# Adding the experts' parts to the output in DRAM by accumulating transfers, with the first product of each half scaled on ScalarE

## The chip, the cores and the metric

One core of one Trainium2 chip. The metric is the device time of one execution in microseconds (us), as the median of several executions. The kernel before takes 1807.9 us (four runs, 1805.82 to 1808.64). The chip is one of several, so each series of runs has its own runs of the kernel before.

Names: PE is TensorE (PEld its weight loads), DVE is VectorE, ACT is ScalarE, POOL is GpSimd, SP is SyncE.

## The reference

```python
# attention without softmax: batch 8, heads 8, sequence 576, head size 64
kv  = einsum('bhsd,bhse->bhde', k, v)
o   = einsum('bhsd,bhde->bhse', q, kv)
x   = o / sqrt(mean(o*o, -1) + 1e-6) * g_norm        # -> 4608 rows x 512
# four experts, all of them applied to every row
p   = domain_probs / (domain_probs.sum(-1) + 1e-9)
out = zeros(4608, 512)
for e in range(4):
    h    = maximum(x @ w1[e], 0)                     # 512 -> 1024
    out += p[:, e:e+1] * (h @ w2[e])                 # 1024 -> 512
```

The change concerns the last line, the sum over the experts.

## The kernel before

The rows are worked in 9 blocks of 512. A step is one expert and one block, so there are 36 steps: first all nine blocks with expert 0, then with expert 1, and so on. Both products of a step are made with seven instead of eight block products (a Strassen form), which costs DVE and POOL many additions. At a *change of expert* the sums of the next expert's weights (`w1y` and `big`, 128x256 each) come on top of the usual additions of the step.

The kernel keeps its own list scheduler. Every operation has a key (its place in the work), a cost for each engine that may do it, and the buffers that it needs. The scheduler simulates the engines, gives each addition to whichever of DVE and POOL can take it first, and emits the instructions in that order. Additions carry a flag, so that the simulation runs them one at a time. That flag does not reach the program: in the emitted program only data dependencies order an addition of one engine against one of the other.

```python
def either(n):
    return {"DVE": 0.17 + 0.00108 * n, "POOL": 0.1 + 0.0025 * n}

def combine(key, cost, out_, a, b, op, reads, writes):      # every addition of the Strassen forms
    plan.add(
        key, cost,
        lambda eng: adder(eng).tensor_tensor(out=out_(), in0=a(), in1=b(), op=op),
        reads=reads, writes=writes, port=True,              # port: one at a time, in the simulation
    )
...
def down(s, e, c):                                          # h @ w2[e], for block c in step s
    h = hidden.pop(s)
    base = s + 1.0
    acc, made = {}, set()
    for i in range(NR):
        acc[i] = Buf("small", f"acc{s}_{i}")
        if e:                                               # load the sum of the experts so far
            load(
                base + (i % 2) * 0.5 - 0.35, acc[i], lambda i=i: acc[i].ap[:],
                out_kept[c, i][:], 256, reads=[kept[c, "o", i]],
            )
            made |= {(i, 0), (i, 1)}

    def merge(key, ps, i, half):                            # 14 a step, all on DVE
        ...
            if fresh:
                nc.vector.tensor_scalar_mul(
                    out=acc[i].ap[:, cols], in0=ps.ap[:, 0:HN], scalar1=prob
                )
            else:
                nc.vector.scalar_tensor_tensor(
                    out=acc[i].ap[:, cols], in0=ps.ap[:, 0:HN], scalar=prob,
                    in1=acc[i].ap[:, cols], op0=ALU.mult, op1=ALU.add,
                )
        ...
    ...                                                     # store: from SP, to out_kept, at the last expert to out
            plan.add(
                key, pe(4, HN), product, reads=[h[m], w2f[e][m]], writes=[ps]
            )
```

Of the kernel before, what the change touches and what calls it, by code (L numbers as in the profile page):

```python
# [10 lines left out]
ALU = mybir.AluOpType  # L11
# [179 lines left out]
def kernel(  # L191
# [30 lines left out]

    nc = tc.nc
# [49 lines left out]
    out_kept = {  # L273
        (c, i): dram.tile([P, DM], F32, tag=f"o{c}_{i}", name=f"o{c}_{i}")
        for c in range(NCH) for i in range(NR)
    }

    plan = Plan()

    def pe(products, columns, passes=2):  # L280
        return {"PE": passes * products * (2 * columns + 6) / 2400 + 0.003}
# [423 lines left out]
    hidden = {}  # L705
    last = []
# [107 lines left out]
    def down(s, e, c):  # L814
        h = hidden.pop(s)
        base = s + 1.0
        acc, made = {}, set()
        for i in range(NR):
            acc[i] = Buf("small", f"acc{s}_{i}")
            if e:  # L820
                load(
                    base + (i % 2) * 0.5 - 0.35, acc[i], lambda i=i: acc[i].ap[:],
                    out_kept[c, i][:], 256, reads=[kept[c, "o", i]],
                )
                made |= {(i, 0), (i, 1)}

        def merge(key, ps, i, half):
            cols = slice(half * HN, (half + 1) * HN)

            def fn(eng):  # L830
                fresh = (i, half) not in made
                made.add((i, half))
                prob = p_all[:, c * NR + i, e:e + 1]
                if fresh:
                    nc.vector.tensor_scalar_mul(  # L835
                        out=acc[i].ap[:, cols], in0=ps.ap[:, 0:HN], scalar1=prob
                    )
                else:
                    nc.vector.scalar_tensor_tensor(  # L839
                        out=acc[i].ap[:, cols], in0=ps.ap[:, 0:HN], scalar=prob,  # L840
                        in1=acc[i].ap[:, cols], op0=ALU.mult, op1=ALU.add,
                    )

            plan.add(key - 0.4, {"DVE": 0.5}, fn, reads=[ps, probs], parts=[acc[i]])

        def store(key, i):
            if e < E - 1:
                kept[c, "o", i] = Buf(None, f"o{c}_{i}")
                plan.add(
                    key, SPC,  # L850
                    lambda eng: nc.sync.dma_start(out=out_kept[c, i][:], in_=acc[i].ap[:]),
                    reads=[acc[i]], writes=[kept[c, "o", i]], kb=256,
                )
                return

            def final(eng):
                if c < B:
                    rows = out[c * S:c * S + NT, :].rearrange("(p r) d -> p r d", r=NR)
                    nc.sync.dma_start(out=rows[:, i, :], in_=acc[i].ap[:])
                    return  # L860
                for bb in range(2):
                    end = (2 * i + bb + 1) * S
                    nc.sync.dma_start(
                        out=out[end - REM:end, :], in_=acc[i].ap[bb * REM:(bb + 1) * REM, :]
                    )

            plan.add(key, SPC, final, reads=[acc[i]], kb=256)

        for t in range(2):
            banks = {}  # L870
            for j, m in enumerate(ORDER):
# [8 lines left out]
                def product(eng, m=m, t=t, ps=ps):  # L880
# [8 lines left out]
                plan.add(  # L889
                    key, pe(4, HN), product, reads=[h[m], w2f[e][m]], writes=[ps]  # L890
                )
                if m in (1, 2):
                    merge(key, ps, t, 0)
                elif m in (6, 3):
                    merge(key, ps, t, 1)
                elif m in (5, 7):
                    merge(key, ps, 2 + t, 1)
                elif m == 4:
                    merge(key, ps, 2 + t, 0)
# [68 lines left out]
```

## Time and profile before

| what | before |
|---|---|
| time, median | 1807.9 us (the profiled execution: 1805.55 us) |
| span of the profile | 1803.8 us |
| PE busy | 1788.7 us, 99% |
| DVE, ACT, POOL busy | 1010.0, 614.3, 582.0 us |
| waits of PE, all | 10.1 us, 8.3 of them in the first 80 us |
| end of PE to end of span | 4.55 us |

PE is the bound, and it loses time where it waits. Three stretches matter below, the three changes of expert. The windows view of the kernel before: the columns are the stretch, its length, then the busy time (and number of instructions) of PE, PEld, DVE, ACT and POOL, the granted PE clock, the share of the DMA engines and GB/s.

```profile
500.00:560.00 60.00, 58.75 (x394) 54.08 (x393) 36.48 (x67) 17.82 (x42) 30.99 (x23) 1.00 0.40 132
...
930.00:970.00 40.00, 40.00 (x270) 37.52 (x269) 24.43 (x45) 12.29 (x27) 14.58 (x11) 1.00 0.55 180
...
1350.00:1410.00 60.00, 60.00 (x402) 56.15 (x401) 37.18 (x62) 20.03 (x43) 30.24 (x16) 1.00 0.51 170
```

Look at the first figure after the length: PE loses 1.25 us at the change to expert 1 and nothing at the other two.

### The profile page before, as it was taken

The numbers are of one execution on the slowest core, as the hardware profiler recorded it, in microseconds if no ns is written. First come the engines' busy times: TensorE is split into PE (matmuls) and PEld (weight loads), VectorE is DVE, ScalarE is ACT, GpSimd is POOL, SyncE is SP. The second block draws the span as 40 slices with busy tenths as digits, with TensorE's granted clock in tenths as the row PEclk, the third lists the DMA queues.
The fourth block names the chain that finished last, engine by engine and source line by source line (L and its number), as shares of the span: only waits on it lengthen the run. The fifth ranks groups of instructions, "written<-read, shape, count | busy, mean of one in ns | idle before, by whom it ended". The sixth has DMA issues, their size and how long they took to land.

```text
span 1803.8 us, 31919 instructions
## 1 busy us (share of the span) xinstructions
PE 1788.7 (99%) x12626; PEld 1667.9 (92%) x12626; DVE 1010.0 (56%) x1757; ACT 614.3 (34%) x1345; POOL 582.0 (32%) x447
## 2 busy tenths in 40 slices
PE   8999999999999999999999999999999999999998
PEld 8899999999989999999999999999999999999997
DVE  5765565556565555555565555555565555555553
ACT  3534444443232333333333333333332333333331
POOL 4855555546445211111155111111144211111112
PEclk9999999999999999999999999999999999999999
DMA  9855454323343333343445333334444334344321
GB/s 229 250 188 138 129 170 154 113 97 141 134 141 129 129 129 129 129 128 123 157 147 169 118 120 127 124 123 129 152 161 167 122 124 129 129 129 129 128 96 35
DMA packets 163286, 247.78 MB, mean 137 GB/s; under 512 B 51009, under 2 KB 92225, under 8 KB 163137
## 3 DMA queue, kind: packets, MB, share of 16 engines
q1 hardware_dynamic: 163136, 245.75, 42.6%
q8 instruction: 99, 1.62, 0.4%
q14 instruction: 51, 0.41, 0.1%
HBM read 172.56 MB, written 73.14 MB: 136 GB/s over the span
## 4 chain that ended last, share of the span: by engine, by line
PE 97%; DVE 1%; POOL 1%; SPq 1%; DMA 0%; ACT 0%; issue 0%; POOLq 0%; DVEq 0%; ACTq 0%
PE u L745 44%; PE db L882 30%; PE ab L882 18%; PE ab L539 1%; PE ab L521 1%; PE ab L549 1%; PE ab L506 1%; SPq L310 1%; PE ab L588 0%; DMA big<-in_v_dram 0%; PE u L927 0%; POOL big L304 0%; DVE big L304 0%; POOL rt L458 0%; PE ab L603 0%
## 5 line engine op out<-in xcount | busy, mean ns | idle before, releaser
L304 POOL TENSOR_TENSOR big<-big,big 128x1024 f32<-128x1024 f32 x136 | 323.7, 2391 | 1005.9 <-DVE big L304 815.0
L882 PE MATMUL db<-big,big 128*128 128x256 f32 x2520 | 594.6, 379 | 0.7 <-POOL big L304 0.7
L882 PEld LDWEIGHTS db<-big,big 128*128 128x128 f32 x2520 | 455.7, 190 | 50.8 <-POOL big L304 1.1
L745 PEld LDWEIGHTS u<-xf,big 128*128 128x128 f32 x3600 | 470.2, 192 | 20.9 <-issue 0.9
L761 ACT ACTIVATE snap<-u 128x256 f32<-128x256 f32 x756 | 290.1, 384 | 585.3 <-PE u L745 497.2
L745 PE MATMUL u<-xf,big 128*128 128x128 f32 x3600 | 486.1, 276 | 0.1
L769 DVE TENSOR_TENSOR big<-u,snap 128x256 f32<-128x256 f32 x756 | 314.8, 422 | 240.0 <-PE u L745 124.0
L304 DVE TENSOR_TENSOR big<-big,big 128x1024 f32<-128x1024 f32 x292 | 372.9, 1278 | 31.4 <-ACT big L728 13.3
L745 PE MATMUL u<-xf,w1y 128*128 128x128 f32 x2700 | 357.1, 275 | 0.7 <-DVE big L769 0.6
L882 PE MATMUL ab<-big,big 128*128 128x256 f32 x1512 | 357.4, 379 | 0.0
L745 PEld LDWEIGHTS u<-xf,w1y 128*128 128x128 f32 x2700 | 334.6, 192 | 5.8 <-DVE big L769 1.0
L882 PEld LDWEIGHTS ab<-big,big 128*128 128x128 f32 x1512 | 273.3, 190 | 29.8
L839 DVE SCALAR_TENSOR_TENSOR small<-db,p_all,small 128x256 f32<-128x256 f32 x243 | 117.2, 482 | 247.6 <-PE db L882 247.3
L761 ACT ACTIVATE big<-u 128x256 f32<-128x256 f32 x252 | 96.8, 384 | 413.3 <-PE u L745 410.9
L728 ACT ACTIVATE big<-big 128x1024 f32<-128x1024 f32 x144 | 151.8, 1054 | 71.7 <-DVE big L304 60.3
L839 DVE SCALAR_TENSOR_TENSOR small<-ab,p_all,small 128x256 f32<-128x256 f32 x189 | 91.1, 482 | 149.5 <-PE ab L882 149.4
L835 DVE TENSOR_SCALAR small<-db,p_all 128x256 f32<-128x256 f32 x72 | 34.7, 482 | 70.3 <-PE db L882 63.9
L458 POOL TENSOR_TENSOR rt<-ss,mhalf 128x8 f32<-128x8 f32 (+1 forms) x40 | 66.1, 1652 | 3.3
L304 POOL TENSOR_TENSOR xf<-xf 128x128 f32<-128x128 f32 (+1 forms) x74 | 47.8, 656 | 17.6 <-DVE xf L304 15.2
L449 DVE TENSOR_REDUCE ss<-small 128x8 f32<-128x512 f32 (+1 forms) x40 | 27.1, 679 | 22.4 <-ACT small L444 22.3
L454 POOL TENSOR_SCALAR ss<-ss 128x8 f32<-128x8 f32 (+1 forms) x40 | 9.3, 232 | 77.2 <-DVE ss L449 75.8
L745 PE MATMUL u<-small,big 128*128 128x128 f32 x216 | 33.6, 280 | 0.6 <-ACT snap L761 0.5
(83 smaller groups left out, 744.3 us busy)
## 6 DMA issues: line engine op xcount, KB each, us to landing
xf<-x SPq DMA_DIRECT2D x108, 512.0 KB, 3.4
o<-small SPq DMA_DIRECT2D x108, 256.0 KB, 2.1
small<-o SPq DMA_DIRECT2D x108, 256.0 KB, 4.2
xf<-x_h SPq DMA_DIRECT2D x81, 256.0 KB, 3.4
xf<-x SPq DMA_DIRECT2D x81, 256.0 KB, 3.6
x<-xf SPq DMA_DIRECT2D x36, 512.0 KB, 3.2
big<-in_moe_w_dram SPq DMA_DIRECT2D x32, 512.0 KB, 5.8
small<-in_q_dram SPq DMA_DIRECT2D x72, 128.0 KB, 4.1
```

What stands on the lines that cost most here:

```text
L304: lambda eng: adder(eng).tensor_tensor(out=out_(), in0=a(), in1=b(), op=op),
L310: key, SPC, lambda eng: nc.sync.dma_start(out=dst(), in_=src), reads=reads,
L449: lambda eng: nc.vector.reduce_sum(out=ss.ap[0:n, :], in_=rows(sq), axis=AX.X),
L458: nc.gpsimd.tensor_tensor(out=rt.ap[0:n, :], in0=ss.ap[0:n, :], in1=mhalf[0:n, :], op=ALU.pow)
L506: nc.tensor.transpose(bank.ap[:, rs], qt.ap[:, rs], ident[:])
L728: lambda eng: nc.scalar.activation(out=b.ap[:], in_=b.ap[:], func=ACT.Relu),
L745: nc.tensor.matmul(ps.ap[:, u * P:(u + 1) * P], lhsT=w1f[e][m][mm][1]()[:, u * P:(u + 1) * P], rhs=views[m][mm][1](), start=(mm in (1, 2, ...
L761: lambda eng: nc.scalar.activation(out=where(), in_=ps.ap[:, 0:HN], func=ACT.Copy),
L769: lambda eng: nc.vector.tensor_tensor(out=block(whole, a, t), in0=src.ap[:, 0:HN], in1=add_.ap[:], op=ALU.add),
L835: nc.vector.tensor_scalar_mul(out=acc[i].ap[:, cols], in0=ps.ap[:, 0:HN], scalar1=prob)
L839: nc.vector.scalar_tensor_tensor(out=acc[i].ap[:, cols], in0=ps.ap[:, 0:HN], scalar=prob, in1=acc[i].ap[:, cols], op0=ALU.mult, op1=ALU.add,)
L882: nc.tensor.matmul(ps.ap[:, 0:HN], lhsT=four(h[m])[:, kt // 2, t, kt % 2, :], rhs=w2f[e][m].ap[:, kt * HN:(kt + 1) * HN], start=(m in (1, ...
```

## The change

The intent is to free the DMA queues and DVE. An expert's part is no longer added to the sum on DVE after loading that sum; it is scaled, and then added to the output in DRAM by the transfer itself. Such transfers are issued from POOL. Since no half starts from a loaded sum, the first product of each half is only a scaling, which ACT can do. A third thing comes with it, in the last hunk: in the second half of a step's down product (`h @ w2[e]`), products 1 and 2 may not come before product 5 (`m == 5`) of the first half (`after=second[-1:]`). Without that line the scheduler finds no order at all for the changed kernel: it stops with "no operation can start".

```diff
-                load(
-                    base + (i % 2) * 0.5 - 0.35, acc[i], lambda i=i: acc[i].ap[:],
-                    out_kept[c, i][:], 256, reads=[kept[c, "o", i]],
-                )
...
+            if fresh:
+                plan.add(
+                    key - 0.4, act(HN),
+                    lambda eng: nc.scalar.activation(
+                        out=acc[i].ap[:, cols], in_=ps.ap[:, 0:HN], func=ACT.Copy, scale=prob()),
+                    reads=[ps, probs], writes=[first], parts=[acc[i]],
+                )
+                return
...
             def fn(eng):
+                for parts, dst in where:
+                    if e:
+                        nc.gpsimd.dma_start(out=dst, in_=acc[i].ap[parts, :], accum_op=ALU.add)
+                    else:
+                        nc.sync.dma_start(out=dst, in_=acc[i].ap[parts, :])
...
-                plan.add(
-                    key, pe(4, HN), product, reads=[h[m], w2f[e][m]], writes=[ps]
-                )
+                op = plan.add(
+                    key, pe(4, HN), product, reads=[h[m], w2f[e][m]], writes=[ps],
+                    after=second[-1:] if t and m in (1, 2) else (),
+                )
+                if m == 5:
+                    second.append(op)
...
-                    merge(key, ps, t, 0)
+                    merge(key, ps, t, 0, m == 1)
```

More of the change, by code (lines that the diff above doesn't have):

```diff
@@ L271 @@
         for c in range(NCH) for m in ("h0", "h1", 1, 2, 3, 4, 5, 6, 7)
-    }
-    out_kept = {
-        (c, i): dram.tile([P, DM], F32, tag=f"o{c}_{i}", name=f"o{c}_{i}")
-        for c in range(NCH) for i in range(NR)
     }
@@ L705 @@
     hidden = {}
+    summed = {}
     last = []
@@ L816, in down @@
         base = s + 1.0
-        acc, made = {}, set()
-        for i in range(NR):
-            acc[i] = Buf("small", f"acc{s}_{i}")
-            if e:
-                load(
-                    base + (i % 2) * 0.5 - 0.35, acc[i], lambda i=i: acc[i].ap[:],
-                    out_kept[c, i][:], 256, reads=[kept[c, "o", i]],
-                )
-                made |= {(i, 0), (i, 1)}
-        def merge(key, ps, i, half):
-            cols = slice(half * HN, (half + 1) * HN)
-            def fn(eng):
-                fresh = (i, half) not in made
-                made.add((i, half))
-                prob = p_all[:, c * NR + i, e:e + 1]
-                if fresh:
-                    nc.vector.tensor_scalar_mul(
-                        out=acc[i].ap[:, cols], in0=ps.ap[:, 0:HN], scalar1=prob
-                    )
-                else:
-                    nc.vector.scalar_tensor_tensor(
-                        out=acc[i].ap[:, cols], in0=ps.ap[:, 0:HN], scalar=prob,
-                        in1=acc[i].ap[:, cols], op0=ALU.mult, op1=ALU.add,
-                    )
-            plan.add(key - 0.4, {"DVE": 0.5}, fn, reads=[ps, probs], parts=[acc[i]])
@@ L846, in store, with merge, prob @@
-        def store(key, i):
-            if e < E - 1:
-                kept[c, "o", i] = Buf(None, f"o{c}_{i}")
+        acc = {i: Buf("small", f"acc{s}_{i}") for i in range(NR)}
+        def merge(key, ps, i, half, fresh):
+            cols = slice(half * HN, (half + 1) * HN)
+            first = halved[i, half]
+            def prob():
+                return p_all[:, c * NR + i, e:e + 1]
+            if fresh:
                 plan.add(
-                    key, SPC,
-                    lambda eng: nc.sync.dma_start(out=out_kept[c, i][:], in_=acc[i].ap[:]),
-                    reads=[acc[i]], writes=[kept[c, "o", i]], kb=256,
+                    key - 0.4, act(HN),
+                    lambda eng: nc.scalar.activation(
+                        out=acc[i].ap[:, cols], in_=ps.ap[:, 0:HN], func=ACT.Copy, scale=prob()),
+                    reads=[ps, probs], writes=[first], parts=[acc[i]],
@@ L853, in store @@
                 )
                 return
-            def final(eng):
-                if c < B:
-                    rows = out[c * S:c * S + NT, :].rearrange("(p r) d -> p r d", r=NR)
-                    nc.sync.dma_start(out=rows[:, i, :], in_=acc[i].ap[:])
-                    return
-                for bb in range(2):
-                    end = (2 * i + bb + 1) * S
-                    nc.sync.dma_start(
-                        out=out[end - REM:end, :], in_=acc[i].ap[bb * REM:(bb + 1) * REM, :]
-                    )
@@ L867, in store @@
-            plan.add(key, SPC, final, reads=[acc[i]], kb=256)
+            plan.add(
+                key - 0.4, {"DVE": 0.5},
+                lambda eng: nc.vector.scalar_tensor_tensor(
+                    out=acc[i].ap[:, cols], in0=ps.ap[:, 0:HN], scalar=prob(),
+                    in1=acc[i].ap[:, cols], op0=ALU.mult, op1=ALU.add,
+                ),
+                reads=[ps, probs, first], parts=[acc[i]],
+            )
+        halved = {(i, f): Buf(None, f"acc{s}_{i}_{f}") for i in range(NR) for f in range(2)}
@@ new lines, in rows, with store, fn @@
+        def rows(i):
+            if c < B:
+                return [(slice(0, P), out[c * S:c * S + NT, :].rearrange(
+                    "(p r) d -> p r d", r=NR)[:, i, :])]
+            ends = [(2 * i + bb + 1) * S for bb in range(2)]
+            return [
+                (slice(bb * REM, (bb + 1) * REM), out[ends[bb] - REM:ends[bb], :])
+                for bb in range(2)
+            ]
+        def store(key, i):
+            where = rows(i)
+            was = summed.get((c, i))
+            now = summed[c, i] = Buf(None, f"o{s}_{i}")
+            def fn(eng):
+                for parts, dst in where:
[3 more added lines that the diff above has]
+                        nc.sync.dma_start(out=dst, in_=acc[i].ap[parts, :])
+            plan.add(
+                key, {"POOL": 1.2 * len(where)} if e else {"SP": 0.55 * len(where)}, fn,
+                reads=[acc[i]] + ([was] if was else []), writes=[now], kb=256,
+            )
@@ L869, in down @@
+        second = []
         for t in range(2):
@@ L887, in product @@
                         )
-                plan.add(
-                    key, pe(4, HN), product, reads=[h[m], w2f[e][m]], writes=[ps]
-                )
+                op = plan.add(
+                    key, pe(4, HN), product, reads=[h[m], w2f[e][m]], writes=[ps],
+                    after=second[-1:] if t and m in (1, 2) else (),
+                )
+                if m == 5:
+                    second.append(op)
                 if m in (1, 2):
-                    merge(key, ps, t, 0)
+                    merge(key, ps, t, 0, m == 1)
                 elif m in (6, 3):
-                    merge(key, ps, t, 1)
+                    merge(key, ps, t, 1, m == 6)
                 elif m in (5, 7):
-                    merge(key, ps, 2 + t, 1)
+                    merge(key, ps, 2 + t, 1, m == 5)
                 elif m == 4:
-                    merge(key, ps, 2 + t, 0)
+                    merge(key, ps, 2 + t, 0, True)
             store(base + 0.5 * (t + 1), t)
```

## The prediction

> **What bounds the kernel now.** I read the page's busy shares first, then its slices, then the chain that ended last, then the waits of TensorE alone, and last the groups that the change touches. From the page:
>
> ```profile
> PE 1788.7 (99%) x12626; PEld 1667.9 (92%) x12626; DVE 1010.0 (56%) x1757; ACT 614.3 (34%) x1345; POOL 582.0 (32%) x447
> ...
> PEclk9999999999999999999999999999999999999999
> DMA  9855454323343333343445333334444334344321
> ...
> PE 97%; DVE 1%; POOL 1%; SPq 1%; DMA 0%; ACT 0%; issue 0%; POOLq 0%; DVEq 0%; ACTq 0%
> PE u L745 44%; PE db L882 30%; PE ab L882 18%; PE ab L539 1%; PE ab L521 1%; PE ab L549 1%; PE ab L506 1%; SPq L310 1%; PE ab L588 0%; DMA big<-in_v_dram 0%; PE u L927 0%; POOL big L304 0%; DVE big L304 0%; POOL rt L458 0%; PE ab L603 0%
> ```
>
> The reader sees a TensorE that is never free, at the full granted clock, while every other engine has 44% or more of the span to spare and the DMA engines have more than half, except in the first slices. Busy matmuls alone would not prove that PE has no slack, so I looked for its waits. The waits of PE list 13 pairs, about 11.4 us in all; limited to stretches of time they lie before 80 us (attention starting up), 1.1 us between 500 and 600 us, 0.7 us near the end, and none at all from 100 to 500 us and from 600 to 1760 us. The windows and the chain in order of time say the same:
>
> ```profile
> 600.00:700.00 100.00, 100.00 (x674) 93.82 (x673) 54.71 (x94) 31.59 (x70) 14.07 (x6) 1.00 0.40 129
> ...
> 1779.33 0.02 issue
> 1779.35 1.06 ACT big L728
> 1780.41 0.03 POOLq L304
> 1780.44 1.20 POOL big L304
> 1781.64 0.04 issue
> 1781.68 1.99 PE db L882 x8
> 1783.68 1.73 PE ab L882 x8
> 1785.40 6.91 PE db L882 x32
> 1792.31 6.92 PE ab L882 x32
> 1799.23 0.02 issue
> 1799.26 0.48 DVE small L839
> ```
>
> The stream is at its own rate. Eight records of a down product take 1.73 us (0.216 each), sixteen of an up product take 1.78 us in the same view (0.111 each). The groups count 4032 down records and 7056 up records: 4032 x 0.216 + 7056 x 0.111 = 871 + 783 = 1654 us of the 1803.8. The rest is attention, the filler matmuls at the start, the 11 us of waits and the end. One of the 36 steps (an expert and a block of rows) is 1654 / 36 = 46 us of PE.
>
> **What the Trainium skill says.** The page "DMA: Bandwidth & Descriptors", section "SWDGE vs HWDGE vs iDMA", says that accumulating in a transfer can only be had from GpSimd, whose cores write the descriptors in software. The trace before has no transfer from POOL (all data goes on SP's queue), so it neither agrees nor disagrees. The same page, "Anatomy of one DMA", fits a GpSimd transfer with 2.0 us plus bytes over 436 GB/s: 2.6 us for 256 KB and 2.3 us for 128 KB. SP's plain stores of those sizes landed in 2.1 to 2.9 us and 2.3 us here, so the size of that figure is plausible; what reading and adding in DRAM costs on top is not in it. "Perfetto Trace Analysis", section "DMA Instruction — SWDGE (GPSIMD)", says that the profiled end of such an instruction is the last descriptor written, not the data landed, so POOL's rows will show its own time, not the transfer's. "SBUF — State Buffer", section "SBUF: two separate sides", says that GpSimd and VectorE exclude each other when VectorE runs a two-port mode, or has two SBUF inputs while GpSimd reads SBUF; it warns of descriptor writing that starves. The trace before cannot test it for descriptors.
>
> **The change part by part.** The groups and issues it touches:
>
> ```profile
> L304 POOL TENSOR_TENSOR big<-big,big 128x1024 f32<-128x1024 f32 x136 | 323.7, 2391 | 1005.9 <-DVE big L304 815.0
> L761 ACT ACTIVATE snap<-u 128x256 f32<-128x256 f32 x756 | 290.1, 384 | 585.3 <-PE u L745 497.2
> L304 DVE TENSOR_TENSOR big<-big,big 128x1024 f32<-128x1024 f32 x292 | 372.9, 1278 | 31.4 <-ACT big L728 13.3
> L839 DVE SCALAR_TENSOR_TENSOR small<-db,p_all,small 128x256 f32<-128x256 f32 x243 | 117.2, 482 | 247.6 <-PE db L882 247.3
> ...
> o<-small SPq DMA_DIRECT2D x108, 256.0 KB, 2.1
> small<-o SPq DMA_DIRECT2D x108, 256.0 KB, 4.2
> ```
>
> *Merges.* Of the 504 merges of a down product (14 per step), 8 per step are the first into their half and go to ACT: 288. DVE loses 288 x 0.482 = 139 us. ACT gains 288 evictions of 128x256 out of PSUM, which take 0.384 us in the group of the same shape: 111 us. A bank is then free about 0.1 us sooner. PE does not wait for banks in the stretches above, so this is worth nothing by itself.
>
> *Work moved.* The order of instructions of the two kernels shows that the scheduler uses DVE's free time: 51 of the 136 large 128x1024 adds go from POOL to DVE, and some forty small ones. POOL loses 51 x 2.391 = 122 us and about 19 us of small ones; DVE gains 51 x 1.278 = 65 us and about 12 us. DVE comes to 1010 - 139 + 65 + 12 = about 950 us, ACT to 725 us, POOL's arithmetic to about 440 us. In a step of expert 1 to 3 POOL keeps one large add where it had three.
>
> *Transfers.* 108 loads of the partial output (28 MB) and 108 stores to a scratch tensor go from SP's queue; 40 plain stores stay (expert 0), and 120 accumulating transfers come to POOL (96 of 256 KB, 24 of 128 KB). I take 1 us of POOL for each, an estimate from the first-byte time of about 1 us on the DMA page (the schedule itself assumes 1.2): 120 us beside the work it lost. In a step that is four issues, about 4 to 5 us, and one add of 2.4 us, in 46 us. Each adding transfer waits for the previous one of the same rows; that one is nine steps, over 400 us, older. Its staging tile is used again about two steps later, some 90 us after the issue. Both are far from any limit.
>
> *PE.* Same 6540 matrix instructions in both programs, same shapes; the order is identical up to the 511th, where the first down products start, so the start-up with most of the waits is untouched. None of the three parts above is on the path that sets the end. Sum for the body: 0.
>
> *The closing step* is different. Before, from the end of PE at 1799.23 to the end of the span are 4.57 us: 0.48 of merge, a short issue, the landing, the closing. The last block is the one whose rows go out in two 64-row transfers, so after the change POOL issues four transfers at the end in order: two for row 1, whose merge is done 1.2 us before PE ends, and two for row 3, whose last product ACT evicts 0.4 us after PE ends. At 0.7 to 1.2 us each (an estimate from the 1 us above, less for half the rows) POOL is done 1.8 to 3.6 us after PE; landing 2.5 to 3.5 us with the addition; closing 0.6. That is 4.9 to 7.7 us where 4.57 were: +0.3 to +3.1, middle +1.7. Against it, the wait of 0.7 us on POOL at 1781 should shrink, as the chain of adds and relus before it gets two DVE adds in place of two POOL adds. Net about +1 us.
>
> **The rivals.**
> 1. *POOL becomes slow or blocked.* If an issue costs 2 us or more, or descriptor writing is starved by DVE (busier with two-input adds), the add that POOL keeps, which an early product of each down part needs, is late in every step. For it: POOL runs in order, and that add stands right behind four issues. Against it: POOL idles 86% of these stretches, and each step has several us between that add and the product. Waits of 0.5 to 1.5 us in 27 steps would make 1822 to 1850 us.
> 2. *ACT or DVE late for the up products.* ACT's merges stand between the evictions that the up products wait for. Against it: 0.384 us each, ACT at 40%, and the scheduler placed them with costs close to the measured ones. At 0.2 us in some 36 steps: +5 to +8 us.
> 3. *The saved traffic pays.* The loads removed could have slowed the block loads of the next step. Against it: PE waits for no transfer after 40 us, so these were hidden; the gain is 0. Even removing every PE wait gives 11 us, 0.6%.
> 4. *Adding transfers are far slower than plain ones.* Hidden in the body; in the closing step 5 to 10 us more.
>
> **Range and chances.** 1808.56 plus 1 is about 1810 us. Downwards only the scatter of the runs before (1805.82 to 1808.64) and a few us of waits are to be had: 1803. Upwards rivals 2 and 4 together give 1822. Faster by over 2% would need 36 us from a TensorE that has 11 us of waits: 1%. Slower by over 2% needs rival 1 in its strong form: 4%.
>
> **What would show it.** Right: PE at 99% with 12626 records, no wait of PE between 100 and 1760 us above 3 us in all, ACT near 725 us, DVE near 950 us, POOL below 460 us of arithmetic, SP without loads of the partial output, a new queue for POOL's transfers, and 5 to 8 us from the last matmul to the end. Wrong: PE waits on POOL or ACT that return in each step of the later experts, or a mean of the large POOL or DVE add far above 2391 and 1278 ns, or issues of POOL over 2 us; then the step "sum for the body: 0" has failed.

## More of the kernel before

One more line turned out to matter, and I had not looked at it before I predicted. It is from the view of the program's closing line, POOL's drain (a wait of the engine for itself at the end); the three numbers are the shortest, median and longest duration in ns, then the first and last start.

```profile
L963 POOLq DRAIN  x3: 39/77/2456, 1781.7 to 1803.5; - x3
```

The longest, 2.46 us from 1781.7, covers POOL's last addition, which takes about 2.35 us. The drain itself costs next to nothing here.

## The result

The changed kernel takes 1822.24 us (four runs, 1821.33 to 1823.74) where the kernel before took 1807.9. The ratio is 1.0082, with a 95% interval of 1.0065 to 1.0099. It is correct. Ratios here are the mean time of one kernel's fast runs over that of the other's of the same rounds, so they are not quite the ratio of the medians. The loss is below 2%, but the 14.3 us are real, and they lie just outside the range.

Line numbers differ a little from kernel to kernel: L304, L300 and L301 are the same line of the additions. From the page of the changed kernel: busy times, queues, bytes of HBM, and the groups that answer to those of the prediction. In a group, the numbers after the bar are the total busy us and the mean ns of one, then the idle time before them. The last line is from the list of issues: count, size, median us to landing.

```profile
PE 1795.1 (99%) x12626; PEld 1672.5 (92%) x12626; DVE 990.0 (54%) x1545; ACT 734.1 (40%) x1633; POOL 564.7 (31%) x491
...
q0 software_dynamic: 15744, 28.32, 10.4%
...
HBM read 144.25 MB, written 73.14 MB: 119 GB/s over the span
...
L300 DVE TENSOR_TENSOR big<-big,big 128x1024 f32<-128x1024 f32 x343 | 465.3, 1359 | 52.6 <-ACT big L725 29.6
...
L862 POOL DMA_DIRECT2D out_dram<-small x120 | 103.4, 889 | 915.6 <-ACT small L827 480.6
...
L827 ACT ACTIVATE small<-db,p_all 128x256 f32<-128x256 f32 x180 | 85.2, 473 | 198.1 <-PE db L885 192.5
...
out_dram<-small POOLq DMA_DIRECT2D x96, 256.0 KB, 5.0
```

The reader is to see that the work moved as intended: 28.32 MB on a new queue, HBM reads down from 172.56 to 144.25 MB, merges on ACT. But the large DVE addition now takes 1359 ns on average where it took 1278.

The same windows as before, now of the changed kernel:

```profile
500.00:560.00 60.00, 57.34 (x371) 52.26 (x371) 34.28 (x64) 21.55 (x48) 19.98 (x14) 1.00 0.38 125
...
930.00:970.00 40.00, 37.93 (x252) 34.95 (x251) 28.54 (x40) 14.44 (x33) 22.26 (x15) 1.00 0.49 137
...
1350.00:1410.00 60.00, 57.38 (x378) 52.92 (x377) 39.33 (x55) 21.97 (x49) 31.21 (x20) 1.00 0.50 131
```

PE lost 0 us in the second and third stretch; now it loses 2.07 and 2.62 (and 2.66 instead of 1.25 in the first). The waits of PE from 920 to 990 us name what it waits for (total us, times, longest). Before, this list is empty.

```profile
PE u L742 <- DVE big L766: 1.0, 2, 0.5
PE ab L885 <- DVE small L834: 1.0, 1, 1.0
PE u L742 <- ACT snap L758: 0.3, 1, 0.3
PE db L885 <- DVE big L300: 0.3, 1, 0.3
```

From 1340 to 1410 us the list is the same, number for number: the loss comes back at each change of expert. Three of the four are late DVE instructions. Why DVE is late shows in the timeline of the changed kernel around 945 us (start, duration, engine, instruction):

```profile
939.41 2.40 POOL L300 TENSOR_TENSOR big<-big,big 128x1024 f32<-128x1024 f32 x1 [1.47 <-DVE big L766]
...
939.51 3.44 DVE L300 TENSOR_TENSOR big<-big 128x256 f32<-128x256 f32 x2
...
944.27 0.41 DVE L300 TENSOR_TENSOR w1y<-big 128x256 f32<-128x256 f32 x1
...
947.87 2.65 POOL L300 TENSOR_TENSOR big<-big,big 128x1024 f32<-128x1024 f32 x1
...
948.14 2.67 DVE L300 TENSOR_TENSOR w1y<-big,w1y 128x256 f32<-128x256 f32 x1
```

A DVE addition of 128x256 takes 0.41 us when POOL is not adding (944.27). The one that began 0.27 us after a POOL addition took 2.67 us and ended 0.29 us after it. Two more took 3.44 us together in the same way. The merge of 943.22 and the evictions behind them come late, and PE waits.

The whole trace of the changed kernel says the same; these counts are worked out from it. The 261 large DVE additions that meet no POOL addition take 1225 ns in the median and 1227 at most; the 80 that overlap one by over 0.1 us take 1743 in the median and up to 3046. Two things do not hold DVE up. Additions with only one input in SBUF and the other in PSUM (`big<-u,snap`) stay at 424 ns in the median, 426 at most, in the 145 cases that lie wholly under a POOL addition. And the 72 large additions that overlap only an issue of POOL take 1225 ns.

The end is the other half. The chain of the last pieces, and the view of the closing line:

```profile
1811.60 0.80 POOL out_dram L862
1812.40 0.84 POOLq L969
```

```profile
L969 POOLq DRAIN  x3: 40/102/9185, 1812.0 to 1821.7; - x3
```

The chain no longer ends in a merge but in POOL's issue of the last rows and then in POOL's sequencer on the closing line. PE ends at 1810.80, POOL's last issue at 1813.24. POOL's drain stands from 1812.01 to 1821.19, and the span ends at 1822.0. So the end takes 11.17 us after the last product where it took 4.55.

**Where the loss lies.** I subtracted from the start of each PE record the start of the record with the same number in the first profile of before, and took the median of that offset in stretches between the changes of expert (records 1500 to 3000, 5400 to 6600, 7700 to 9400, 10600 to 12100; the order of PE differs in places, hence the median). The differences between stretches are what each change of expert costs. This table is worked out from the traces; all in us.

| kernel | start | change to expert 1 | to expert 2 | to expert 3 | last step | end of PE to end of span |
|---|---|---|---|---|---|---|
| before (first profile) | 0 | 0 | 0 | 0 | 0 | 4.55 |
| before_again | 1.72 | 0.00 | 0.01 | 0.00 | 0.00 | 4.55 |
| after | 2.73 | 2.05 | 3.74 | 3.73 | -0.67 | 11.17 |
| a_port | 5.44 | 3.68 | 0.10 | 0.08 | -0.67 | 11.15 |
| b_tail | 3.52 | 2.03 | 3.73 | 3.71 | 0.62 | 4.94 |
| c_sp_plain | 1.34 | 2.04 | 2.21 | 2.19 | -0.66 | 4.54 |
| g_both | 3.87 | 3.70 | 0.09 | 0.08 | 0.62 | 4.96 |
| d_dve_first | 3.18 | 2.44 | 0.42 | 0.41 | 0.62 | 11.11 |
| f_pool_plain | 3.38 | 2.03 | 3.32 | 3.30 | -0.66 | 12.49 |
| e_before_port | 2.08 | -0.54 | -0.20 | -0.21 | 0.00 | 4.54 |
| h_all | 2.38 | 2.03 | 0.09 | 0.08 | 0.09 | 4.92 |
| i_xf | 0.91 | 2.28 | 0.09 | 0.08 | 0.09 | 4.95 |
| j_before_late | 1.48 | -0.54 | -0.20 | -0.21 | 0.00 | 4.55 |
| k_second | 1.02 | 2.44 | 0.26 | 0.25 | 0.56 | 4.54 |

The row "after" without its start sums to 2.05 + 3.74 + 3.73 - 0.67 + (11.17 - 4.55) = 15.5 us. The start is mostly spread: the first profile of before was an execution of 1805.55 us, 2.3 below the median, and that of after one of 1823.74, 1.5 above its own. So 15.5 + 2.7 - 2.3 - 1.5 = 14.4 us, against 14.3 between the medians. Three parts of it had to be explained: the end (6.6), the changes to experts 2 and 3 (3.7 each), and the change to expert 1 (2.05). At expert 2 the table has 3.7 us where the list of waits has 2.6. The rest follows the waits: eight records of a down product take 1.99 us right after a wait (943.74) and 1.73 in the running stream (936.18), so each of the five waits costs some 0.2 us more than its gap.

### The profile page after: what moved, and what is told of

Read it like the earlier page. It is cut to its first block, busy times and chain, and to the rows that moved or that the text cites. A ratio compares the mean times of both kernels' runs of the same rounds, so it can differ in the third digit from the quotient of the medians.

```text
span 1822.0 us, 31844 instructions
## 1 busy us (share of the span) xinstructions
PE 1795.1 (99%) x12626; PEld 1672.5 (92%) x12626; DVE 990.0 (54%) x1545; ACT 734.1 (40%) x1633; POOL 564.7 (31%) x491
## 3 DMA queue, kind: packets, MB, share of 16 engines
q0 software_dynamic: 15744, 28.32, 10.4%
HBM read 144.25 MB, written 73.14 MB: 119 GB/s over the span
## 4 chain that ended last, share of the span: by engine, by line
PE 95%; DVE 3%; issue 1%; POOL 1%; ACT 0%; DMA 0%; SPq 0%; POOLq 0%; DVEq 0%; ACTq 0%
PE u L742 42%; PE db L885 30%; PE ab L885 17%; DVE big L300 1%; PE ab L535 1%; PE ab L517 1%; PE ab L502 1%; PE ab L545 1%; PE u L933 1%; PE ab L584 0%; DVE big L766 0%; DVE w1y L300 0%; POOL rt L454 0%; DMA small<-in_q_dram 0%; PE db L535 0%
## 5 line engine op out<-in xcount | busy, mean ns | idle before, releaser
L300 DVE TENSOR_TENSOR big<-big,big 128x1024 f32<-128x1024 f32 x343 | 465.3, 1359 | 52.6 <-ACT big L725 29.6
L862 POOL DMA_DIRECT2D out_dram<-small x120 | 103.4, 889 | 915.6 <-ACT small L827 480.6
L742 PE MATMUL u<-xf,w1y 128*128 128x128 f32 x2700 | 353.3, 276 | 2.1 <-DVE big L766 1.1
L300 POOL TENSOR_TENSOR big<-big,big 128x1024 f32<-128x1024 f32 x85 | 207.7, 2449 | 126.9 <-DVE big L300 39.3
L827 ACT ACTIVATE small<-db,p_all 128x256 f32<-128x256 f32 x180 | 85.2, 473 | 198.1 <-PE db L885 192.5
L834 DVE SCALAR_TENSOR_TENSOR small<-db,p_all,small 128x256 f32<-128x256 f32 x135 | 65.2, 483 | 143.5 <-PE db L885 141.4
L827 ACT ACTIVATE small<-ab,p_all 128x256 f32<-128x256 f32 x108 | 51.2, 474 | 186.1 <-PE ab L885 186.0
L834 DVE SCALAR_TENSOR_TENSOR small<-ab,p_all,small 128x256 f32<-128x256 f32 x81 | 39.0, 481 | 58.8 <-PE ab L885 58.8
L300 POOL TENSOR_TENSOR xf<-xf 128x128 f32<-128x128 f32 (+1 forms) x62 | 43.3, 708 | 14.8 <-DVE xf L300 13.7
```

Of the source, the lines that this page charges most:

```text
L742: nc.tensor.matmul(ps.ap[:, u * P:(u + 1) * P], lhsT=w1f[e][m][mm][1]()[:, u * P:(u + 1) * P], rhs=views[m][mm][1](), start=(mm in (1, 2, ...
L827: lambda eng: nc.scalar.activation(out=acc[i].ap[:, cols], in_=ps.ap[:, 0:HN], func=ACT.Copy, scale=prob()),
L834: lambda eng: nc.vector.scalar_tensor_tensor(out=acc[i].ap[:, cols], in0=ps.ap[:, 0:HN], scalar=prob(), in1=acc[i].ap[:, cols], op0=ALU.mu ...
L862: nc.gpsimd.dma_start(out=dst, in_=acc[i].ap[parts, :], accum_op=ALU.add)
```

## The experiments

Theory at the outset: DVE and POOL additions hold each other up and make PE wait at the changes of expert, and POOL's transfers lengthen the end. Rivals: POOL's time for issuing, the adding in the transfers, and the merges on ACT.

### a_port: the additions wait for each other

```diff
 def combine(key, cost, out_, a, b, op, reads, writes):
+    def fn(eng):
+        new = adder(eng).tensor_tensor(out=out_(), in0=a(), in1=b(), op=op)
+        if ported and ported[-1][0] != eng:
+            tc.add_manual_dep(new.ins, ported[-1][1].ins.name, ...)   # a real wait on the other engine's last addition
+        ported.append((eng, new))
```

> The changed kernel with the same order of instructions on every engine, but each add that was scheduled behind an add of the other of DVE and POOL now really waits for it. Theory 1 (adds of DVE and POOL that overlap hold each other up; in the changed kernel single DVE adds of 128x256 took 1.6 to 2.7 us there instead of 0.42, merges came late, and PE waited some 9 us in all around the three changes of expert): the large DVE add comes back from 1359 to about 1235 ns mean, the PE waits between 500 and 1450 us nearly go, and the time falls by 6 to 10 us to about 1813 to 1816. Theory 2 (POOL's issues of accumulating transfers stand in the way of POOL's adds): the waits stay, 1822 +-2. Theory 3 (the new order itself gives PE too little slack): the waits stay or grow, 1822 to 1830.

Measured: 1819.61 us, ratio 1.0067 (1.0052 to 1.0082), correct. The 3.7 us at experts 2 and 3 fell to 0.1 each, and the large addition became quick again. Its group in this kernel:

```profile
L301 DVE TENSOR_TENSOR big<-big,big 128x1024 f32<-128x1024 f32 x343 | 419.1, 1224 | 104.5 <-POOL big L301 47.0
```

That is the same 343 additions at 1224 ns, where the changed kernel had 1359. What follows: the overlap of the two engines' additions is the cause at experts 2 and 3. But forcing them apart cost 1.6 us more at the change to expert 1, and the start is 2.7 us later (some of that may be spread, see before_again), so the time fell by only 2.6, where 6 to 10 had been expected.

### b_tail: the last step as before

```diff
+        old = s == E * NCH - 1             # last step: load the sum, merge on DVE, store from SP
+            fresh = fresh and not old
...
-                    if e:
+                    if e and not old:
                         nc.gpsimd.dma_start(out=dst, in_=acc[i].ap[parts, :], accum_op=ALU.add)
```

> The changed kernel, but only the last step (expert 3, last rows) works as before the change: partial sums loaded, all merges on DVE, stores from SP. Theory 1 (the end is 6.6 us longer because four issues of POOL follow one another after the last product and because POOL's closing drain, 9.2 us long in the profile, ended 5 us after the last data had landed): the time from the last matmul to the end of the span falls from 11.2 to 4.5 to 5.5 us, and the time by 5.5 to 7 us to about 1816. Rival (the closing drain costs its 8 to 9 us after any use of transfers from POOL, whenever they ended): the end stays above 9 us and the time above 1820.

Measured: 1818.65 us, 1.0063 (1.0048 to 1.0078), correct. The end fell from 11.17 to 4.94 us, as theory had it; 1.3 us of that came back as a new wait of PE on POOL in the last step, and the time fell by 3.6, where 5.5 to 7 had been expected. The drain of POOL did not become shorter, it only moved:

```profile
L980 POOLq DRAIN  x3: 40/93/9329, 1792.4 to 1817.5; - x3
```

It now starts at 1792.4, 20 us before PE ends, and nobody waits for it. POOL's last transfer had landed at 1790.77, before this drain even began, so its 9.3 us are no wait for data to land.

### c_sp_plain: plain stores from SP

```diff
-                        nc.gpsimd.dma_start(out=dst, in_=acc[i].ap[parts, :], accum_op=ALU.add)
+                        nc.sync.dma_start(out=dst, in_=acc[i].ap[parts, :])
```

> Wrong result on purpose (plain stores, so only the last expert's part stays in the output). Same order on PE, DVE and ACT, same adds on POOL; the 120 accumulating transfers of POOL are plain stores issued by SP. Theory 1: the end comes back to 4.5 to 5.5 us after the last matmul, but the PE waits around the changes of expert stay, because the adds of DVE and POOL still overlap: about 1815 to 1817. Theory 2 (POOL's issues delay its adds, or the accumulation itself disturbs the other transfers): the waits around the changes of expert go as well, about 1806 to 1809.

Measured: 1813.14 us, 1.0032 (1.0017 to 1.0047), wrong result; the time lies below the 1815 to 1817 of the theory and above the 1806 to 1809 of its rival, and each has a part. The end is that of before (4.54 us), and experts 2 and 3 cost 2.2 us each instead of 3.7. POOL's issuing, which stands between its additions, thus carries about 1.5 of the 3.7, and the rest needs no transfer from POOL at all. The drain without any transfers of POOL:

```profile
L969 POOLq DRAIN  x3: 40/82/2452, 1783.7 to 1810.6; - x3
```

### g_both: a and b together

The edit is that of a_port and that of b_tail.

> Both mends together: adds of DVE and POOL made to wait for each other, and the last step as before the change. Theory 1, both parts right and additive: 1822 - 6 to 10 - 6 = 1806 to 1810, the same as the kernel before within 0.2%. If only one part is right, 1813 to 1817.

Measured: 1814.36 us, 1.0037 (1.0021 to 1.0054), correct. The expected 1806 to 1810 was missed. The two gains add up in the table (0.09, 0.08, 4.96), but the costs of a_port at expert 1 (3.70) and some of those at the start remain, and 0.62 us come in the last step. The pair of additions that stood on top of each other at 948 us in the changed kernel now follow each other, in the timeline of this one:

```profile
949.68 0.42 DVE L301 TENSOR_TENSOR w1y<-big,w1y 128x256 f32<-128x256 f32 x1
...
950.19 2.35 POOL L301 TENSOR_TENSOR big<-big,big 128x1024 f32<-128x1024 f32 x1 [0.51 <-DVE w1y L301]
```

2.65 beside 2.67 us have become 0.42 and then 2.35.

### d_dve_first: the first products scaled on DVE again

```diff
-                    key - 0.4, act(HN),
-                    lambda eng: nc.scalar.activation(
-                        out=acc[i].ap[:, cols], in_=ps.ap[:, 0:HN], func=ACT.Copy, scale=prob()),
+                    key - 0.4, {"DVE": 0.5},
+                    lambda eng: nc.vector.tensor_scalar_mul(
+                        out=acc[i].ap[:, cols], in0=ps.ap[:, 0:HN], scalar1=prob()),
```

> The changed kernel, but the first product of each half is scaled on DVE as before the change (288 evictions back from ACT to DVE); the accumulating transfers from POOL stay. The scheduler then leaves 291 large adds to DVE and 137 to POOL, as before the change (292 and 136), instead of 343 and 85. Theory 1 (freeing DVE made the scheduler move 51 large adds to it, in an order whose adds overlap with POOL's on the chip): mean of the large DVE add near 1280 ns, PE waits around the changes of expert at most 1 us each, the end still 11 us after the last matmul; about 1813 to 1816. Theory 2 (POOL's issues between its adds are what makes them overlap): POOL now has both more adds and the issues, so the waits stay or grow: 1820 to 1828.

Measured: 1817.58 us, 1.0058 (1.0043 to 1.0073), correct; 1.6 us above the range of the theory, as the change to expert 1 (2.44) and the last step (0.62) cost more than in the changed kernel. Experts 2 and 3 cost 0.4 us each, though POOL still issues all its transfers. DVE does 291 large additions again instead of 343. So it is the move of the merges to ACT that sets off most of the overlap there: the scheduler fills the freed DVE with additions. That these 52 additions themselves are the ones that collide is argued, not shown.

### f_pool_plain: transfers from POOL that do not add

```diff
-                        nc.gpsimd.dma_start(out=dst, in_=acc[i].ap[parts, :], accum_op=ALU.add)
+                        nc.gpsimd.dma_start(out=dst, in_=acc[i].ap[parts, :])
```

> Wrong result on purpose (the stores do not add, so only the last expert's part stays). Same order on every engine as the changed kernel, same 120 transfers from POOL, but plain. If the addition in DRAM costs time: landing well below the 5.0 us of the adding ones, the end shorter by about that difference (1 to 3 us), 1819 to 1821. If it is POOL as the issuer that costs (issues one after the other, and the closing drain): same waits, same drain of about 9 us, 1821 to 1823. I expect the second.

Measured: 1823.6 us, 1.0089 (1.0072 to 1.0105), wrong result. The line of issues and the drain in this kernel:

```profile
out_dram<-small POOLq DMA_DIRECT2D x96, 256.0 KB, 2.9
```

```profile
L969 POOLq DRAIN  x3: 40/102/10486, 1811.8 to 1822.8; - x3
```

Landing fell from 5.0 to 2.9 us for 256 KB, and the mean issue on POOL from 0.86 to 0.54 us (the group's busy time over its 120). The time did not fall. The adding is therefore at most a small part of the loss: experts 2 and 3 cost 0.4 us less each, with the shorter issues, and the end took more than that back. It grew to 12.49 us although the data land sooner.

### e_before_port: the kernel before, with its additions apart

The edit is that of a_port, in the kernel before.

> A control: the kernel before the change with its own order, and the adds of DVE and POOL made to wait for each other as scheduled. It has few overlaps that matter (large DVE add 1278 ns mean, PE waits of 1.1 us between 500 and 600 us and 0.2 us later), so by theory 1 the mean falls to about 1225 ns and the time changes by -1 to +3 us; the three or so us that the same waits cost at the start in the changed kernel (PE waiting on DVE in the attention part) may return here. If it came out 5 us or more faster, the overlap would be a cost of the kernel before as well.

Measured: 1807.95 us, 1.0003 (0.9988 to 1.0018), correct. The kernel before has some of the overlap too: its changes of expert become cheaper by 0.54, 0.20 and 0.21 us, and its large DVE addition falls from 1278 to 1224 ns. In the time it is not seen.

### h_all: the repairs together

```diff
-            if ported and ported[-1][0] != eng:
+            if key > NCH + 0.5 and ported and ported[-1][0] != eng:      # from the middle of expert 1's first step on
...
-                key, either(2 * NT), lambda: to.ap[:], lambda: a.ap[:], lambda: b.ap[:], op,
+                key, (dve if key > E * NCH - 0.2 else either)(2 * NT),   # the last step's late additions on DVE alone
```

On top of this it has the last step of b_tail.

> The changed kernel with what the first runs point to: adds of DVE and POOL wait for each other only from expert 1 on (no cost at the start, where the full version lost 2.7 us, nor at the first change of expert, where it lost 0.9), the last step as before the change, and the last adds of that step on DVE (with the last step alone as before, PE waited 1.3 us for POOL there). Theory 1: changes to expert 2 and 3 cost under 1 us in all, the end is 5 us, the start and the first change keep their 2 us: 1808 to 1811. It would not be clearly faster than the kernel before, since PE has nothing more to lose.

Measured: 1810.45 us, 1.0017 (1.0002 to 1.0032), correct. Of the 14.3 us, 3.0 are left against the runs of before beside it (1807.47). The table has 2.7 of them: 2.03 us at the change to expert 1, 0.4 at the end, and 0.26 at the other three places.

### i_xf: the late forms of the input moved to POOL

```diff
 def x_forms(c, key):
+    cost = gp if c == NCH - 1 else either      # last block: POOL alone
```

> The version h_all, whose last 2.0 us of loss appear at the change to expert 1, with one thing moved: the six adds of the input's forms for the last block, which in h_all sat on VectorE behind a weight add that a POOL add had stretched to 1.25 us (TensorE waited 1.13 us for the last of them), are on POOL alone, in the same place in its order. TensorE's order of products is unchanged. Theory: the late forms make the better part of the 2.05 us, so the offset at the change to expert 1 against the first profile of before falls by some 1.1 us to about 1.0, and the median from 1810.45 to some 1809.3. Rival: TensorE waits there for evictions and snapshots of ACT as well, and one wait that goes lets the next one come out; the offset stays at about 2.0 and the median at 1810.4.

Measured: 1810.36 us, 1.0018 (1.0004 to 1.0031), correct. The theory missed. PE's wait of 1.0 us for these forms on DVE became one of 1.2 us for them on POOL, and the change to expert 1 cost 2.28 us. In the trace POOL's six forms (4.03 us from 520.20) run at the same time as DVE's sums of the weights (519.27 to 522.6). That this is why the wait stayed is argued, not shown.

### j_before_late: the kernel before, additions apart except at the start

```diff
-            if ported and ported[-1][0] != eng:
+            if key > 2 and ported and ported[-1][0] != eng:
```

> The kernel before, with its adds on VectorE and POOL made to wait for each other only after the first two orders of the start (e_before_port had them wait from the beginning, which cost about 2 us at the start and gave 0.5 back at the change to expert 1). Theory: the start offset goes back to that of before, the gain of 0.5 us at the change to expert 1 is kept, so the time is 1807.0 against 1807.5, a ratio of 0.9997. Rival: the start offset of 2 us was only the run-to-run spread of the start, and the time is again that of before, 1807.5 to 1808.

Measured with five rounds: 1806.13 us against 1806.98, 0.9996 (0.9982 to 1.0009), correct. The trace shows the 0.95 us gained at the three changes. The interval includes 1, so a version faster than before is not shown. The start came out at 1.48 us, within the spread that before_again shows, so the theory about the start is not decided.

### before_again: the kernel before once more

The edit is none.

> The kernel before, unchanged, profiled once more: how far the start of one and the same kernel moves from one execution to the next. Theory: the first profile of before (span 1803.8 us) was a lucky start, and this one has its products some 1 to 3 us later from the first 100 us on, with the same offsets from there and no loss at the changes of expert. Rival: within 0.5 us of the first profile everywhere, so that the start offsets of 2.4 to 3.9 us of the changed versions are costs of the change.

Measured: 1807.28 us in one execution, state unknown as there was only one. Its products are 1.72 us later than in the first profile from the start on and then stay there to 0.01 us. Start offsets up to about 2 us therefore say nothing about a change.

### k_second: the kernel before, with the order of the second half alone

```diff
                 op = plan.add(
                     key, pe(4, HN), product, reads=[h[m], w2f[e][m]], writes=[ps],
+                    after=second[-1:] if t and m in (1, 2) else (),
                 )
+                if m == 5:
+                    second.append(op)
```

> The kernel before with one line of the change alone: TensorE's second half of each down-projection may not begin its first two products before the fifth product of the first half, as in the changed kernel. Its merges, loads and stores are those of before. It is the one thing that every version with a loss of 2.0 to 2.4 us at the change to expert 1 had in common and that touches TensorE's order already in expert 0. Theory: the order it makes the scheduler choose brings the input's forms next to the weight sums at that change, and the products are 2.0 us later from there on; about 0 at the other two changes; 1809 against 1807. Rival: the loss comes from something that this leaves out (the loads of the partial output that are gone, and with them other moments at which buffers come free); the offset at the change to expert 1 is within 0.3 us of 0 and the time is that of before.

Measured: 1810.43 us, 1.0021 (1.0004 to 1.0038), correct. The change to expert 1 costs 2.44 us, exactly as in d_dve_first, and PE waits there for the same things as in the changed kernel. Its waits from 500 to 560 us:

```profile
PE u L745 <- ACT snap L761: 1.3, 3, 0.5
PE u L745 <- DVE xf L304: 1.0, 1, 1.0
PE u L745 <- DVE big L769: 0.2, 1, 0.2
```

In the kernel before, this stretch has two entries and none on `xf`:

```profile
PE u L745 <- DVE big L769: 0.6, 2, 0.3
PE u L745 <- ACT snap L761: 0.5, 1, 0.5
```

In the changed kernel they are the three of k_second, with the same totals. The loss at expert 1 thus needs neither the transfers nor the merges on ACT: the one ordering line brings it. In the kernel before, POOL begins the forms of the last block (`xf`) at 506.0 us; here it begins at 519.5, together with the weight sums. The first line is of the kernel before, the others are of k_second:

```profile
506.01 1.27 POOL L304 TENSOR_TENSOR xf<-x_rem,xf 128x512 f32<-128x512 f32 x1 [7.89 <-PE u L745]
...
519.47 1.26 POOL L304 TENSOR_TENSOR xf<-x_rem,xf 128x512 f32<-128x512 f32 x1 [6.91 <-PE u L745]
519.77 1.25 DVE L304 TENSOR_TENSOR w1y<-big 128x256 f32<-128x256 f32 x1
```

The DVE sum next to the form of POOL takes 1.25 us instead of 0.41, so additions hold each other up here too. But making them wait (a_port, 3.68) or moving the forms (i_xf, 2.28) did not help: how much of the 2 us each of the three waits is worth stays open.

## Why the prediction was right or wrong

**What bounds the kernel: right.** PE stayed at 99% with 12626 records, and the time moved by under 1%. The 28 MB of loads that are gone gave nothing, so rival 3 (the saved traffic pays) fell as argued. The 11.4 us of PE's waits are a slip: the 13 entries add up to 10.0, 10.1 in the trace. That changes nothing in the argument. A wait does cost some 0.2 us more than its entry, which the prediction could not see in a kernel with hardly any.

**Merges: right in kind, mis-sized.** ACT took 473 ns for one, not the 384 of the eviction of the same shape that I had borrowed, so 288 x 0.473 = 136 us and not 111. It cost PE nothing that these runs show: with the merges on ACT, experts 2 and 3 cost 0.1 us each in a_port. That ACT's busy time still came within 9 us of the 725 is partly luck: records that follow each other at once overlap, so the sum of ACT's durations rose by 134.8 us but its busy time by 119.8.

**Work moved: nearly right.** DVE came to 990 us (about 950 predicted), ACT to 734 (725), POOL's arithmetic to 564.7 - 103.4 = 461 (440). The first gap is largely the held-up additions: 343 x (1359 - 1278) = 28 us of the 40.

**Transfers: right on POOL, nearly right on landing.** An issue took 0.86 us of POOL (1 predicted). Landing took 5.0 us for 256 KB; the run without adding took 2.9, so the adding costs about 2.1 us. The prediction's estimate of 2.6 us, from the Trainium skill's page "DMA: Bandwidth & Descriptors", section "Anatomy of one DMA", is close to the plain 2.9. The last four transfers, of 128 KB each, landed 3.1 to 4.1 us after their issue began and the last one 3.0 us after its issue ended, where 2.5 to 3.5 had been predicted. No experiment shows that the landing costs any time.

**"Sum for the body: 0" failed.** It was 2.05 + 3.74 + 3.73 = 9.5 us, from two things that the step left out.
- 7.5 us: I moved 51 large additions from POOL to DVE and multiplied each by its own mean, as if the engines ran side by side. I had cited from the Trainium skill's page "SBUF — State Buffer", section "SBUF: two separate sides", that the two exclude each other when VectorE has two inputs in SBUF, but used it only for descriptor writing. The trace agrees with that statement where it counts: 0.41 us alone, 2.67 us when started under a POOL addition. The mean of 1278 ns already held some of this; apart, the same addition takes 1224 (e_before_port).
- 2.05 us: the ordering line is in the diff, and none of my parts priced it. I had seen that PE's order differs from the 511th instruction on and took the new order to be as good (k_second).

I had named no wait above 3 us in all between 100 and 1760 us as the sign of being right. In the changed kernel they come to 2.5 us at expert 1 and 2.6 at each of the other two, 7.7 in all and all at the changes of expert, where the sums of the weights are added to what DVE and POOL have to do.

**The closing step: mechanism half right, size wrong.** Predicted +0.3 to +3.1, middle +1.7; measured +6.6. The terms of its sum were four issues, landing, closing. The issues were in range: POOL is done 2.44 us after PE (1.8 to 3.6 predicted). But landing is not what comes next. POOL's drain lasts until 7.95 us after its last issue (1813.24 to 1821.19), and the closing needs 0.8. The term "landing 2.5 to 3.5 us with the addition" was about right in size but is not on the path; the drain has to stand in its place. The last data landed at 1816.24, 5.4 us after PE; with 0.6 for closing that would have been an end of about 6.0 us (an estimate), inside the 4.9 to 7.7 of the prediction. f_pool_plain (landing sooner, drain longer) and b_tail (drain begun after the landing) show that it isn't the landing; b_tail also shows that an earlier end of POOL's work hides it. Why the drain takes that long stays open. The credit of 0.7 us was paid (-0.67 in the last step).

**The rivals.** Rival 1 named the right pair of engines, but the wrong victim: additions, not descriptors, and three places, not 27 steps. c_sp_plain gives POOL's issuing a share of about 1.5 of each 3.7 us. Rival 2 is contradicted at experts 2 and 3, where PE's wait on ACT is 0.3 of 2.6 us, and at expert 1 the same waits on ACT come without any merge on ACT (k_second). Rival 4 gave "5 to 10 us more" in the closing step, which is the size that came, but through the drain and not through adding.

**Range.** The upper edge of 1822 was set by rivals 2 and 4 together. Neither acted as told; what did act came to 1822.24, just above it.

## What to carry to other kernels

When a change frees VectorE, ask what the scheduler will put there: additions with both inputs in SBUF did not run side by side on VectorE and GpSimd here, and a plan that takes them one at a time must also emit the waits. The waits have a price of their own (3.7 us at expert 1 in a_port), so put them where the overlap costs more, as h_all does. Price every line of a diff that changes the order of TensorE's work, also one that moves no data. If GpSimd issues transfers, let its last work end well before the end of the kernel (its drain stood 7 to 10 us after that in these runs), or give the last stores to another queue.

## What the Trainium skill lacked or had wrong

- The Trainium skill's page "VectorE: DVE Perf Modes", section "The DRAIN you can't avoid", knows a flush after VectorE's operations and boilerplate drains of about 12 ns on all engines. POOL's drain on the program's closing line is like neither: it took 9.2 us after, 9.3 in b_tail and 10.5 in f_pool_plain, all with transfers from POOL, and about 2.45 us, most of it POOL's last addition, without any (before, c_sp_plain). After POOL's last instruction it still stands 7.95 us (after), 6.95 (b_tail) and 9.87 (f_pool_plain). Why it does is open; it does not wait for the data to land.
- "DMA: Bandwidth & Descriptors", section "Anatomy of one DMA", has no term for adding in the transfer: 5.0 us against 2.9 for 256 KB, 0.86 us against 0.54 of POOL for an issue, and 15744 packets against 8832 on the queue for the same 28.32 MB (after and f_pool_plain).
- None of the pages that I read says that the profile's count of bytes read from HBM leaves out what an adding transfer reads. It fell by 172.56 - 144.25 = 28.3 MB, the size of the loads removed, though the adding transfers move 28.32 MB and each has to read what it adds to; f_pool_plain, which adds nothing, shows the same 144.25 MB.
